# Feed-forward weights 7 and 10 in the residual rows' buffers, `wo` in four transfers: a fused attention and feed-forward block on one core

## The chip, the cores and the metric

The kernel runs on one core of a Trainium2 chip. The metric is the device time of one execution in microseconds, lower is better. The core has TensorE (PE in the profile), VectorE (DVE), ScalarE (ACT), GpSimd (POOL) and SyncE (SP), which here only issues transfers; ACT issues some transfers too. Every engine works through its own instructions in order.

## The reference

With `x` of 2048 rows by 512 columns, 32 heads of width 16, and F = 1792:

```
xn  = layernorm(x)
q, k, v = split(xn @ wqkv)                  # 512 x 1536
s   = softmax over 8 keys (rows t, t-2, ..., t-14) of q.k / 4, applied to v, then @ wo
g   = silu(relu(xn @ w1 + b1)^2 @ w2 + b2)  # w1 512 x 1792, w2 1792 x 512
out = x + s * g
```

All inputs and the output are float32; `wqkv`, `wo`, `w1` and `w2` are read from HBM once.

## The kernel before, in words

**Precision.** A matmul operand is kept as two parts, a rounded high part and the low remainder. `split` makes them: a copy on ACT (`high`) and a subtraction on the engine that is named (`low`). A product is three matmuls: high by high, high by low, low by high (`PASSES`).

**First stage (to about 136 us).** The 16 row tiles are normalised and transposed, and q, k and v are computed and stored to HBM scratch (`sq`, `sk`, `sv`). A generator, `attention`, runs the windowed attention on DVE beside everything else: eight units of 256 rows, loaded on ACT's queue (`start`, `load_u`), multiplied and reduced in pieces of about 2.3 us, and stored by SP to scratch `so` (`store`). The v tile of a unit is overwritten with the result, so ACT issues the load of the next unit's v only when that store has landed.

**Order.** Two clocks, one for PE and one for DVE, are advanced at build time by the cost of each traced instruction. `pump(margin)` traces pieces of attention until DVE's clock reaches PE's plus the margin; `defer` and `flush` put loads at a PE time. Compute instructions keep the traced order on their engine. Transfers issued through the plain `dma` on SP are not held to the traced order: a scheduler places them, each with a semaphore wait for its buffer. All transfers share eight semaphores in turn, whichever queue issues them, so a transfer also waits until the one eight before it has landed.

**Second stage (from about 136 us).** The feed-forward block runs in four chunks `c` of 512 rows. Hidden columns come in 14 blocks `f` of 128. `up(c, f)` is 12 matmuls into a PSUM tile `ph` (two buffers, `psH`), then on ACT a relu, a square rounded to `h`'s high part, and a square in full. In chunk 0 and for `f` 2 to 11, the full square goes back into `ph` and DVE makes `h`'s low part from it (`lowh`), which is what frees the `ph` buffer for `up(c, f + 2)`. `down` adds block `f - 2` into four accumulators `pb`.

**Weights.** In chunk 0 each block's weights must still be made. `load_w(f)` fetches raw `w1` and `w2` columns of block `f` into two tiles of tag `z` (four buffers, so two blocks' worth). `next_w`, called once after each `up(0, f)`, splits the next block: two copies on ACT, two subtractions on POOL; then it calls `load_w` for the block two further on, into the buffers that the subtractions free. Blocks 0 to 4 are split in the first stage, block 5 after `up(0, 2)`, block 13 after `up(0, 10)`.

**Output.** `wo` is fetched raw into two tiles `rwo` of tag `oT` (rows in an order that suits 32-column transposes) and split into `wot`. `load_o(u, force)` reads unit `u` of the attention back as `oq` in eight transfers of 64 KB. `trans_o` transposes a tile of it on DVE into PSUM, ACT copies the high part into `oT`, and `lowo` makes the low part on DVE. `out_product` is the 12 matmuls with `wot`. `gate` applies silu; `finish` multiplies and adds the residual rows `xr`, which `load_r` fetched into two buffers of tag `xr`. In chunk 0 the two `oT` tiles take the buffers of the two `rwo` tiles, and `xr` is not used before block 9.

The pool `p2`, with the tags `wot`, `oT`, `oq`, `xr` and the weight tiles of blocks 11 to 13, is opened after the pools of the first stage are closed and lies where they lay. In the profile nearly all compute instructions have line L91, the helper that records them, so tiles tell them apart; transfers have lines of their own: L404 and L405 `load_w`, L986 `wo`, L922 `load_o`, L954 `load_r`, L339 `store`, L104 the ordered queue.

Of the kernel before, what the change touches and what calls it, by code (L numbers as in the profile page):

```python
# [9 lines left out]
F32 = mybir.dt.float32  # L10
# [5 lines left out]
P = 128  # L16
S = 2048
D = 512
F = 1792
KT = D // P  # L20
NF = F // P
# [20 lines left out]
HOME = {0: 10, 1: K0, 2: T1, 3: T2, 4: T3, 5: Q0, 6: Q1, 7: K1, 8: T4, 9: V0, 10: V1}  # L42

SEVEN = range(4, 16, 2)
VSEVEN = range(6, 14, 2)

WARM = 18
# [12 lines left out]
def body(ctx: ExitStack, tc: tile.TileContext, x, wqkv, wo, w1, b1, w2, b2, out):  # L60
# [34 lines left out]
    PE, V, A, G = Ordered(nc.tensor, "PE"), Ordered(nc.vector, "V"), Ordered(nc.scalar), Ordered(nc.gpsimd)  # L95
# [4 lines left out]
    dma = nc.sync.dma_start  # L100

    def queue(out, in_):

        tc.keep_in_program_order(dma(out, in_))  # L104
# [19 lines left out]
    def piece(name):  # L124
        return keep.tile([P, 512], F32, name=name, tag="z", bufs=4)

    def high(hi, lo, src):
        A.activation(hi, src, AF.Copy)

    def low(hi, lo, src, eng):  # L130
        eng.tensor_sub(lo, src, hi.bitcast(F32))

    def split(hi, lo, src, eng):
        high(hi, lo, src)
        low(hi, lo, src, eng)
# [20 lines left out]
    def buffer(name, i):  # L156
        return wts.tile([P, 2, 2, 512], FR, name=name, tag=f"b{i}")
# [87 lines left out]
    def flush(t):  # L245
        while behind and (t is None or behind[0][0] <= t):
            behind.pop(0)[1]()
# [137 lines left out]
    def pump(margin=-SLACK):  # L385

        limit = clock["PE"] + margin
        flush(clock["PE"])
        while True:
            if coming[0] is None:  # L390
                coming[0] = next(stream, None)
            if coming[0] is None or clock["V"] + coming[0] > limit:
                break
            coming[0] = next(stream, None)
        if coming[0] is None:
            not_before(limit)
# [2 lines left out]
    w12 = {}  # L399

    def load_w(f):
        r1, r2 = (piece(f"{n}{f}") for n in ("w1r", "w2r"))
        send = queue if f < 2 else dma
        send(r1.rearrange("p (k c) -> p k c", c=P), w1[:, f * P:(f + 1) * P].rearrange("(k p) c -> p k c", p=P))  # L404
        send(r2, w2[f * P:(f + 1) * P, :])  # L405
        raws[f] = r1, r2

    def next_w():

        f = len(w12)  # L410
        if f < NF:
            w12[f] = buffer(f"w{f}", HOME[f]) if f in HOME else p2.tile([P, 2, 2, 512], FR, name=f"w{f}")
            for i, r in enumerate(raws.pop(f)):
                split(w12[f][:, 0, i], w12[f][:, 1, i], r, G)
            if f + 2 < NF:
                load_w(f + 2)


    NT = S // P
# [316 lines left out]
    for a in range(2, NT, 2):  # L736
        n, t = {2: 2, 4: 1}.get(a, 0), a + 2
        seven = t in SEVEN
        for i in (t, t + 1):
# [25 lines left out]
    for i in range(2):  # L765
        at(4, i, load_w, i)
# [28 lines left out]
    def pair_of_seven(a):  # L795

        b, last = a + 1, a + 2 == NT
        seven = a in VSEVEN
        for s in (1, 2, 0):
# [80 lines left out]
    for a in range(2, NT, 2):  # L880
        if a >= TPC:
            for t in (a, a + 1):
                queue(sx[t // TPC][:, :, t % TPC], xts[t].bitcast(F32))
        (pair_of_seven if a in SEVEN else pair)(a)
        if a == NT - 4:
# [6 lines left out]

    p2 = ctx.enter_context(tc.tile_pool(name="p2", bufs=1))
    pws, gs, pbs = {}, {}, {}

    def begin(c, j):

        pbs[c, j] = psA(f"pb{c}_{j}")
        A.activation(pbs[c, j], b2t, AF.Copy)
# [12 lines left out]
    def load_o(u, force):  # L912

        if u in oqs or (done_units[0] <= u and not force):
            return
        while done_units[0] <= u:
            flush(None)
            pump(clock["V"] - clock["PE"] + 4000)
        oqs[u] = p2.tile([P, UP // 64, 2, 2, CH], F32, name=f"oq{u}", tag="oq")
        for g in range(GR):  # L920
            src = so[g, u * UP:(u + 1) * UP, :].rearrange("(b p e) c -> p b (e c)", p=32, e=2)
            dma(oqs[u][32 * (g // 2):32 * (g // 2) + 32, :, g % 2].rearrange("p b e c -> p b (e c)"), src)  # L922
# [29 lines left out]
    def load_r(t):  # L952
        xrs[t] = p2.tile([P, D], F32, name=f"xr{t}", tag="xr", bufs=2)
        dma(xrs[t], tile_rows(x, t))  # L954
# [9 lines left out]
    wot = p2.tile([P, 2, 4, 512], FR, name="wot")  # L964
    rwo = {}

    for c in range(NCH):
        last = c == NCH - 1
        if c == 0:
            for j in range(TPC):  # L970
                begin(c, j)
        pb = [pbs[c, j] for j in range(TPC)]
        t0 = c * TPC
        room = ROOM if c else ROOM0
        for f in range(2, NF):
            up(c, f)
            if c == 0:
                next_w()
            pump()
            if c == 0 and f in (3, 6):  # L980

                i = f // 6
                rwo[i] = p2.tile([P, 2, D], F32, name=f"rwo{i}", tag="oT", bufs=2)
                for q in range(4):
                    rows = wo[q * P + 64 * i:q * P + 64 * i + 64, :].rearrange("(g p) n -> p g n", g=2)
                    dma(rwo[i][32 * q:32 * q + 32], rows)  # L986
            if c == 0:
                if 6 <= f < 10:
                    split(wot[:, 0, f - 6], wot[:, 1, f - 6], rwo[(f - 6) // 2][:, (f - 6) % 2], G)
            elif f == 2:  # L990
                finish(t0 - 4, G)
            elif f == 3:
                finish(t0 - 3, G)
                load_r(t0 - 2)
                load_r(t0 - 1)
                trans_o(t0 - 2, psT(f"pT{t0 - 2}"))
                trans_o(t0 - 1, psT(f"pT{t0 - 1}"))
            elif f == 4:
                lowo(t0 - 2)
                lowo(t0 - 1)  # L1000
            elif f == 5:
                out_product(t0 - 2, psT(f"pw{t0 - 2}"))
            elif f == 6:
                finish(t0 - 2, G)
                out_product(t0 - 1, psT(f"pw{t0 - 1}"))
            elif f == 7:
                finish(t0 - 1, G)
            if f == 2 and c:
                load_o(c * 2 - 1, True)
            elif f >= 7:  # L1010
                load_o(c * 2, f >= 9)
            if f in (9, 10) and not last:
                load_r(t0 + f - 9)
            if f == 10:
                for i in range(2):
                    trans_o(t0 + i, psT(f"pT{t0 + i}"))
            if f == 11:
                for i in range(2):
                    lowo(t0 + i)
            if f == 11 or (last and f > 11):  # L1020
                load_o(c * 2 + 1, f > 12)
            downs = [f - 2]
            if last and f == NF - 1:
                downs = []
            elif not last and f > NF - 3:
                downs = [f - 3, f - 2] if f == NF - 1 else []
            for i in downs:
                for j in range(TPC):
                    down(pb, i, j)
            pump(room)  # L1030
            lowh(f)
        out_product(t0, psT(f"pw{t0}"))
        if last:
            out_product(t0 + 1, psT(f"pw{t0 + 1}"))
        pump(room)
        if not last:
            for j in range(TPC):
                for i in range(2):
                    down(pb, NF - 2 + i, j)
                pump(room if j < 2 else -SLACK)  # L1040
                gate(c, j, pb)
                begin(c + 1, j)
            for i in range(2):
                up(c + 1, i)
                pump(ROOM)
                lowh(i)
                load_o(c * 2 + 1, False)
            out_product(t0 + 1, psT(f"pw{t0 + 1}"))
            pump(ROOM)
        else:  # L1050
            for i in range(2, TPC):
                trans_o(t0 + i, psH(f"pT{t0 + i}"))
            for i in range(2, TPC):
                lowo(t0 + i)
            xl = xTa.tile([P, TPC, 512], F32, name="xlast", tag="xT")
            dma(xl.rearrange("p (h e) n -> p h (e n)", e=2),
                x[t0 * P:(t0 + TPC) * P, :].rearrange("(h p e) n -> p h (e n)", p=P, e=2))
            for j in range(TPC):
                for f in range(NF - 3, NF):
                    down(pb, f, j)  # L1060
                gate(c, j, pb)
                if j < 2:
                    finish(t0 + j, V, xl[:, j])
            for j in range(2, TPC):
                n = D // 2 if j == TPC - 1 else D
                for i in range(0, D, n):
                    cols = slice(i, i + n)
                    out_product(t0 + j, (psT if i else psH)(f"pw{t0 + j}_{i}"), cols)
                    finish(t0 + j, V, xl[:, j], cols)
# [21 lines left out]
```

## Time and profile before

| | |
|---|---|
| Median of 3 runs | 485.32 us (484.97 to 486.93) |
| Profiled execution | 485.13 us, of which the span is 483.1 us |
| Granted TensorE clock | 1.000 |
| Busy share of the span: PE, DVE, ACT, POOL | 99%, 88%, 50%, 47% |
| Data moved | 81.47 MB, mean 169 GB/s |

The page gives the busy time of each engine, the chain of work that ended last, and groups of instructions by tile. Times in the views are microseconds from the start of the span. The profiled execution's own time is 2.0 us more than its span; the steps below are counted against the profiled execution.

### The profile page before, as it was taken

What the parts mean: (1) busy time and instruction counts of PE and PEld (TensorE: products, weight loads), DVE (VectorE), ACT (ScalarE), POOL (GpSimd) and SP (SyncE); (2) the same over time, 40 slices, a digit from 0 to 9 for tenths busy, and PEclk for the clock granted to TensorE, in tenths of its full rate; (3) what the DMA queues carried; (4) which work ended last, traced back from release to release, by engine and by line L of the source; (5) the groups of instructions that cost most, each with busy time, mean ns of one, the idle gap of its engine ahead of it and who ended that gap; (6) DMA issues with size and microseconds to landing.
All of it is one profiled execution on the core that took longest, in us unless ns stands there. A gap on an engine that the chain in (4) does not pass through costs nothing.

```text
span 483.1 us, 6128 instructions
## 1 busy us (share of the span) xinstructions
PE 477.4 (99%) x2190; PEld 396.6 (82%) x2190; DVE 423.0 (88%) x352; ACT 240.0 (50%) x441; POOL 225.3 (47%) x178
## 2 busy tenths in 40 slices
PE   8999999999999999999999999999999999999996
PEld 5888888888888888888888888888888888888885
DVE  5978999899499899999999999999999999889133
ACT  5548798856566565273513345342234543423240
POOL 1459853116986699436543322434433345253210
PEclk9999999999999999999999999999999999999999
DMA  7899999998779996571627548071707725220321
GB/s 283 243 251 258 277 243 302 263 306 269 209 198 228 255 224 151 178 166 43 170 72 185 115 164 190 26 189 43 197 16 196 224 48 145 43 86 27 87 105 71
DMA packets 71002, 81.47 MB, mean 169 GB/s; under 512 B 6204, under 2 KB 55612, under 8 KB 70972
## 3 DMA queue, kind: packets, MB, share of 16 engines
q1 hardware_dynamic: 65788, 54.87, 41.3%
q10 hardware_dynamic: 5184, 26.22, 21.8%
q8 instruction: 17, 0.28, 0.2%
q14 instruction: 13, 0.11, 0.1%
HBM read 50.60 MB, written 27.32 MB: 161 GB/s over the span
## 4 chain that ended last, share of the span: by engine, by line
PE 98%; DMA 1%; DVE 0%; POOL 0%; issue 0%; ACT 0%; POOLq 0%
PE ph L91 32%; PE pb L91 32%; PE pm L91 12%; PE pq L91 9%; PE pw L91 9%; PE pv L91 4%; DMA x<-in_A_x 1%; PE pxT L91 0%; DVE z L91 0%; DVE st L91 0%; POOL rs L91 0%; DVE xn L91 0%; ACT xT0f L91 0%; DVE mv L91 0%; DVE rs L91 0%
## 5 line engine op out<-in xcount | busy, mean ns | idle before, releaser
L91 PE MATMUL pb<-w,h 128*128 128x512 f32 x672 | 160.1, 389 | 0.0
L91 PEld LDWEIGHTS pb<-w,h 128*128 128x128 f32 x672 | 126.1, 188 | 26.2
L91 POOL TENSOR_TENSOR h<-hf,h 128x512 fp32r<-128x512 f32 x46 | 67.7, 1473 | 157.5 <-ACT hf L91 157.5
L91 PE MATMUL ph<-xU,w 128*128 128x512 f32 x504 | 120.2, 389 | 0.0
L91 ACT ACTIVATE ph<-ph,b1t 128x512 f32<-128x512 f32 x56 | 37.0, 661 | 153.9 <-PE ph L91 144.0
L91 PEld LDWEIGHTS ph<-xU,w 128*128 128x128 f32 x504 | 94.6, 188 | 19.6
L91 DVE TENSOR_TENSOR pr<-k,q 128x2048 f32<-128x2048 f32 x32 | 78.7, 2460 | 3.2 <-DMA q<-sq 2.5
L91 DVE TENSOR_TENSOR pv<-v,L 128x2048 f32<-128x2048 f32 x32 | 77.3, 2417 | 3.8 <-POOL L L91 3.1
L91 DVE TENSOR_REDUCE L<-pr 128x128 f32<-128x2048 f32 x32 | 73.0, 2281 | 0.7
L91 DVE TENSOR_REDUCE v<-pv 128x256 f32<-128x2048 f32 x32 | 72.9, 2279 | 0.7
L91 PE MATMUL pw<-wot,oT 128*128 128x512 f32 (+1 forms) x204 | 45.9, 376 | 0.0
L91 PEld LDWEIGHTS pw<-wot,oT 128*128 128x128 f32 x204 | 36.8, 188 | 7.1
L91 POOL TENSOR_TENSOR w<-w1r,w 128x512 fp32r<-128x512 f32 x14 | 31.6, 2259 | 23.4 <-ACT w L91 23.2
L91 PE MATMUL ph<-xT,w 128*128 128x512 f32 x168 | 40.0, 389 | 0.0
L91 PEld LDWEIGHTS ph<-xT,w 128*128 128x128 f32 x168 | 31.5, 188 | 6.6
L91 PE MATMUL pm<-wq,S 128*128 128x512 f32 x144 | 36.8, 392 | 0.0
L91 ACT ACTIVATE h<-ph 128x512 fp32r<-128x512 f32 x56 | 33.5, 599 | 1.8
L91 PE MATMUL pq<-wq,xT 128*128 128x512 f32 x132 | 30.9, 393 | 0.0
L91 PEld LDWEIGHTS pm<-wq,S 128*128 128x128 f32 x144 | 26.2, 188 | 5.3 <-DVE S L91 0.4
L91 PEld LDWEIGHTS pq<-wq,xT 128*128 128x128 f32 x132 | 24.5, 188 | 5.9 <-ACT xT L91 0.7
L91 ACT ACTIVATE hf<-ph 128x512 f32<-128x512 f32 x46 | 27.4, 595 | 1.9 <-POOL h L91 1.9
L91 PE MATMUL pm<-wq,xt 128*128 128x512 f32 x108 | 27.6, 392 | 0.0
(96 smaller groups left out, 531.0 us busy)
## 6 DMA issues: line engine op xcount, KB each, us to landing
k<-sk ACTq DMA_DIRECT2D x8, 960.0 KB, 7.1
v<-sv ACTq DMA_DIRECT2D x8, 960.0 KB, 7.4
sx<-xt SPq DMA_DIRECT2D x12, 512.0 KB, 5.8
xU<-sx ACTq DMA_DIRECT2D x12, 512.0 KB, 5.9
x<-in_A_x SPq DMA_DIRECT2D x16, 256.0 KB, 6.4
sk<-stg SPq DMA_DIRECT2D x8, 512.0 KB, 4.3
sq<-stg SPq DMA_DIRECT2D x8, 512.0 KB, 7.5
sv<-stg SPq DMA_DIRECT2D x8, 512.0 KB, 5.0
```

The lines of the kernel that those rows point to most:

```text
L91: return tc.keep_in_program_order(f(*a, **k))
```

## The change

Five edits, all for chunk 0 of the second stage:

- Raw weights of blocks 7 and 10 get tiles of tag `xr` in place of tag `z`. Block 7 is fetched as soon as `p2` is open, block 10 after the split of block 7.
- The order of the fetches in `next_w` follows from that: up to block 4, the split of `f` is followed by the fetch of `f + 2`; splits 5 to 9 are followed by the fetch of `f + 3` (8 to 12), split 10 by none, split 11 by block 13.
- `wo` comes in four transfers of 256 KB over 128 partitions in place of eight of 128 KB over 32 partitions. Each has a hand-written source pattern: 4 groups, 32 rows, 512 elements. The second tile is fetched at block 5 in place of 6.
- `wo` is split at blocks 9, 10 and 11 (one, one and two quarters) in place of one quarter at each of 6 to 9.
- The first `load_o` is tried from block 9 (forced from 10) in place of 7 (9); the first two `trans_o` move from block 10 to 12 and their `lowo` from 11 to 13.

```diff
+SPARE = 7, 10
...
     def load_w(f):
-        r1, r2 = (piece(f"{n}{f}") for n in ("w1r", "w2r"))
+        spare = f in SPARE
+        r1, r2 = (p2.tile([P, 512], F32, name=f"{n}{f}", tag="xr", bufs=2) if spare else piece(f"{n}{f}")
+                  for n in ("w1r", "w2r"))
...
-            if f + 2 < NF:
-                load_w(f + 2)
+            after = f + (2 if f < SPARE[0] - 2 or f > 10 else 3)
+            if after < NF and f != 10:
+                load_w(after)
...
     p2 = ctx.enter_context(tc.tile_pool(name="p2", bufs=1))
     pws, gs, pbs = {}, {}, {}
+    load_w(SPARE[0])
...
-            if c == 0 and f in (3, 6):
+            if c == 0 and f in (3, 5):
-                i = f // 6
+                i = f // 5
                 rwo[i] = p2.tile([P, 2, D], F32, name=f"rwo{i}", tag="oT", bufs=2)
-                for q in range(4):
-                    rows = wo[q * P + 64 * i:q * P + 64 * i + 64, :].rearrange("(g p) n -> p g n", g=2)
-                    dma(rwo[i][32 * q:32 * q + 32], rows)
+                for g in range(2):
+                    row = wo[64 * i + 32 * g:64 * i + 32 * g + 1, :]
+                    dma(rwo[i][:, g], bass.AP(tensor=row.tensor, offset=row.offset, ap=[[P * D, 4], [D, 32], [1, D]]))
             if c == 0:
-                if 6 <= f < 10:
-                    split(wot[:, 0, f - 6], wot[:, 1, f - 6], rwo[(f - 6) // 2][:, (f - 6) % 2], G)
+                for q in {9: (0,), 10: (1,), 11: (2, 3)}.get(f, ()):
+                    split(wot[:, 0, q], wot[:, 1, q], rwo[q // 2][:, q % 2], G)
...
-            elif f >= 7:
-                load_o(c * 2, f >= 9)
+            elif f >= (7 if c else 9):
+                load_o(c * 2, f >= (9 if c else 10))
...
-            if f == 10:
+            if f == (10 if c else 12):
                 for i in range(2):
                     trans_o(t0 + i, psT(f"pT{t0 + i}"))
-            if f == 11:
+            if f == (11 if c else 13):
                 for i in range(2):
                     lowo(t0 + i)
```

## The prediction

> **What bounds the kernel now.** I read the page first, then who PE waited for, then the chain of waits in order of time.
>
> ```profile
> PE 477.4 (99%) x2190; PEld 396.6 (82%) x2190; DVE 423.0 (88%) x352; ACT 240.0 (50%) x441; POOL 225.3 (47%) x178
> ...
> PE 98%; DMA 1%; DVE 0%; POOL 0%; issue 0%; ACT 0%; POOLq 0%
> ```
> ```profile
> PE warm L91 <- POOL mhalf L91: 1.4, 1, 1.4
> PE pxT L91 <- DVE xn L91: 0.3, 1, 0.3
> PE pq L91 <- ACT xT0f L91: 0.2, 1, 0.2
> ```
> ```profile
> 5.78 0.46 PE pxT L91 x2
> ...
> 163.59 2.72 PE ph L91 x12
> ...
> 169.03 2.72 PE ph L91 x12
> ...
> 179.91 2.72 PE ph L91 x12
> ...
> 190.79 5.44 PE ph L91 x24
> ...
> 201.67 2.72 PE pw L91 x12
> 204.39 5.44 PE pb L91 x24
> ...
> 473.67 5.60 PE pw L91 x36
> ```
>
> PE runs without a break from 5.78 us to 479.27 us (473.67 + 5.60). Its waits sum to 1.9 us, all of them in kinds of instruction that belong to the start. The change adds and removes no matmul, so it can gain nothing where it acts: the profiled execution's 485.13 us (0.2 us under the median of the runs shown, 485.32) is the floor for it. The question is only whether one of the things that are just in time for PE becomes late. Blocks of the chain that I use: `up(0, 7)` starts at 163.59, 8 at 169.03, 10 at 179.91, 12 at 190.79, 13 at 193.51, and the first output product at 201.67.
>
> What stands close to PE in this stage is read from the windows and the timelines.
>
> ```profile
> 136.00:158.00 22.00, 22.00 (x99) 18.21 (x98) 19.76 (x13) 13.86 (x26) 15.46 (x10) 1.00 0.95 231
> 158.00:180.00 22.00, 22.00 (x99) 18.22 (x98) 21.47 (x12) 13.79 (x25) 19.11 (x11) 1.00 1.01 241
> 180.00:201.00 21.00, 21.00 (x94) 17.41 (x93) 20.79 (x16) 10.49 (x19) 16.80 (x10) 1.00 0.58 152
> ```
>
> The last two columns are the share of the DMA engines and GB/s. From 136 to 180 us the 16 DMA engines have no free time (0.95, 1.01), and DVE has almost none (21.47 of 22). So a transfer that takes longer on an engine delays what is queued behind it there.
>
> **The edits with cover.** First those whose cost I put at nothing.
>
> ```profile
> 142.88 0.37 SPq L404 DMA_DIRECT2D w1r<-in_B_w  x1
> ...
> 145.68 1.41 SPq L986 DMA_DIRECT2D rwo<-in_A_wo  x3
> ...
> 150.14 4.60 SPq L986 DMA_DIRECT2D rwo<-in_A_wo  x2
> 155.12 0.57 SPq L339 DMA_DIRECT2D so<-v  x1
> 157.01 0.38 SPq L404 DMA_DIRECT2D w1r<-in_B_w  x1
> ...
> 180.38 0.33 SPq L405 DMA_DIRECT2D w2r<-in_B_w  x1
> ```
> ```profile
> SPq L986 <- DMA sq<-stg: 1.1, 1, 1.1
> ```
> ```profile
> w1r<-in_B_w SPq DMA_DIRECT2D x14, 256.0 KB, 4.3
> w2r<-in_B_w SPq DMA_DIRECT2D x14, 256.0 KB, 3.6
> ...
> rwo<-in_A_wo SPq DMA_DIRECT2D x8, 128.0 KB, 9.2
> ```
>
> Block 7's fetch. In the trace of before the first transfer into `p2` is the first `rwo`, and it waited for the store `sq<-stg` of the first stage until 145.68. Block 7's raw tiles are now the first into `p2`, so I expect them at about 145.7 and not at 142.88: later, though the edit asks for earlier. Landed after 4.3 us they are there at 150.0, after 9.2 us, as `rwo` did in the same stage, at 154.9.
>
> ```profile
> 151.73 0.62 ACT L91 ACTIVATE w<-w1r 128x512 fp32r<-128x512 f32 x1
> ...
> 161.98 0.52 ACTq L91 DMA_DIRECT2D v<-sv  x1
> 162.61 0.66 ACT L91 ACTIVATE ph<-ph,b1t 128x512 f32<-128x512 f32 x1 [2.06 <-DMA so<-v]
> ...
> 163.79 0.59 ACT L91 ACTIVATE ph<-ph 128x512 f32<-128x512 f32 x1
> ```
> ```profile
> 158.43 2.29 DVE L91 TENSOR_TENSOR pr<-k,q 128x2048 f32<-128x2048 f32 x1 [2.46 <-DMA q<-sq]
> ...
> 166.23 0.68 DVE L91 TENSOR_TENSOR h<-ph,h 128x512 fp32r<-128x512 f32 x1
> ...
> 184.28 1.30 DVE L91 STREAM_TRANSPOSE pT<-oq 128x512 f32<-128x512 f32 x2
> ...
> 188.26 1.27 DVE L91 TENSOR_TENSOR oT<-pT,oT 128x512 fp32r<-128x512 f32 x2
> ```
>
> ACT comes to block 7's split at 151.73, so it waits 0 to 3.2 us. Queued behind it on ACT are the softmax's exponential and the next relu; DVE, which waits for the exponential, sits idle 2.46 us for q until 158.43 anyway. Value taken 0; without that cover about 1 us. Blocks 8 to 12 are fetched one step of 5.44 us (169.03 to 163.59) ahead of before, which only adds slack.
>
> The `wo` splits (one copy and one subtraction each, four of them) move from blocks 6 to 9 to blocks 9 to 11.
>
> ```profile
> 186.13 1.29 POOL L91 TENSOR_TENSOR wot<-rwo,wot 128x512 fp32r<-128x512 f32 x1
> ...
> 188.43 1.30 POOL L91 TENSOR_TENSOR w<-w1r,w 128x512 fp32r<-128x512 f32 x1
> ...
> 199.97 2.83 POOL L91 TENSOR_TENSOR h<-hf,h 128x512 fp32r<-128x512 f32 x1 [1.82 <-ACT hf L91]
> ```
>
> POOL does the same four subtractions of 1.29 us, now behind block 13's weights, and has done them some 5 us after `up(0, 11)` ends at 188.07, that is by 193; they are read at 201.67. Cost 0.
>
> Transposes two blocks later. In before they ran at 184.28, 1.65 us after `up(0, 10)` ended (179.91 + 2.72 = 182.63). Behind `up(0, 12)`, which ends at 193.51, they run at about 195.2 to 196.5; `lowo` follows `up(0, 13)`, end 196.23, and is done by about 199. The product that reads it starts at 201.67, so 2.7 us are left of 13. The two `oT` copies of ACT then stand ahead of the last relu and squares of the chunk, and delay POOL's subtraction of block 13 (end 202.80) by up to 1.5 us; PE reads that at 205.5 (204.39 + five matmuls of 2.72 / 12: three of block 12 for the first accumulator, two of block 13). Cost 0; if DVE is 3 us behind, the product waits, 1 to 3 us. The eight `oq` transfers move ten us later with their readers and leave the full stage; `xr` is needed in chunk 1 only.
>
> **The edit without cover: `wo`.** No transfer of before shows how the new one runs: its source pattern starts with a dimension of 4 (the four groups of rows), where all others start with 14 or more. Bounds. From below, it runs like `w2r`, 256 KB in rows of 2 KB, 3.6 us, spread evenly, and four such are no more work than the eight of before: cost 0, and four issues less on SP (the eight took 9.2 us each to land). From above, it is spread along its outermost dimension, over four of the 16 engines. At 241 GB/s an engine moves 15.1 kB a us; 262 kB on four engines is 65.5 kB each, 4.35 us a transfer and 17.4 us for four, against 4.35 us for all eight of before. That is 13.0 us more on four engines that have nothing free.
>
> The Trainium skill, in DMA: Bandwidth & Descriptors, under "Why a DMA increments its semaphore by 16 and not by 1", says that a transfer runs on the largest number of engines up to 16 that divides the slowest dimension of both patterns, which would be 4 here. No row above can show it. The same page's Rules for kernel authors speak for the edit, one transfer over 128 partitions in place of several over a part of them; by that alone the sum would be 0.
>
> I take the upper spread, because in the code the four groups are the dimension that a split would cut first. What is late then? The store of attention unit 0 (`so<-v`, issued at 155.12) stands behind `wo` on the same queue. ACT stops at the load of the next v until that store has landed; in before this ended at 161.9 and cost ACT 2.06 us. Ahead of the store stood five of the eight `wo` transfers, 5 x 0.54 = 2.7 us of each engine; now at least the first pair, 8.7 us, so 6.0 us more, and block 9's weights, before at 157.01 and now a step earlier, 2.2 us more. The store lands at 161.9 + 8.2 = 170.1 us. From the issue of v, ACT's last square of block 6 ends 2.4 us later (163.79 + 0.59 - 161.98), and DVE's `lowh`, 0.68 us, frees `ph` at 170.2 + 3.1 = 173.3. `up(0, 8)` wants it at 169.03: PE waits 4.3 us. Without the weights' share it is 2.1 us; with the second pair ahead of the store as well, 8.7 us more, 13.0. On the other path, block 13's weights: before, their `w1` half was ready at 189.73 for 193.51, 3.8 us of slack, so 13.0 us more on four engines cost at most 9.2 there, and the wait at block 8 already covers part of it. PE's later work follows at its own pace and nothing later gives time back. Sum: 485.13 + 4.3 = 489.4 us.
>
> **The rivals.**
>
> Hidden, not slower: the `wo` transfers are spread over all engines, or over four that run faster while the other twelve rest, and the store lands before about 165.8, from where it decides (165.8 + 0.1 + 3.1 = 169.0). For it: in the next window the share is 0.58. Against: 1.01 at the store. PE stays unbroken, 485.1 us. The first half of this is also the case in which the change does what it says and relieves the queue.
>
> Late transposes: even with `wo` harmless, the oT low part comes after 201.67 because DVE runs behind the plan by more than 2.7 us; it was 1.65 behind at 184.28. PE waits 1 to 3 us at the product: 486 to 488, taken 487.6.
>
> Faster: would need a break of PE that the profiled execution does not show; 485.1 less at most 1.9 us of waits at the start, which the change doesn't touch.
>
> **How the numbers follow.** A difference of 0.5% (2.4 us) is about what a measurement of this kernel can tell from no change. Four engines and a stall, likeliest, 489.4: 0.66, of which 0.04 stays under 2.4 us. Hidden, 485.1: 0.29. Late transposes, 487.6: 0.04, three quarters of it over the bound. Faster: 0.01. So slower 0.65, within 0.5% 0.34, faster 0.01. The range must hold both main cases: it starts at 484.8, a little under the fastest run of before (484.97), and ends at 494.3, the 9.2 us of the second path; the 13.0 us of a second pair ahead of the store is left out. The likeliest case alone is 487.2 (2.1 us) to 494.3.
>
> **What would show it.** Right: `rwo` lands far later than 9.2 us; ACT waits for `so<-v` to about 170; the first break in PE is at `ph` around 169 us, released by DVE's `h`; DVE's `h<-ph,h` of block 6 is late by the same. A late block 7 shows as ACT at `w` for `w1r` around 152. Wrong: PE unbroken with ACT's wait for `so<-v` near 2 us, or the first break elsewhere, at `pw` (transposes), or at `ph` for POOL's `w` (weights).

## The result and the profile after: 497.5 us, 2.5% slower

The changed kernel takes 497.5 us (median of 6 runs, 496.15 to 500.95) against 485.43 us of before in the same series (484.97 to 486.93): a ratio of 1.0251, 95% interval 1.0215 to 1.0286. Slower, as forecast, but by 12.1 us where 4.3 were forecast, and above the range. The profiled execution took 497.22 us, its span 495.4 us, 12.3 more than before's 483.1. Transfers now have the lines L407 and L408 (`load_w`), L991 (`wo`), L340 (`store`), and the helper is L92.

The page of after: engines, DMA packets, and the chain that ended last; below it, before's DMA packets.

```profile
PE 480.3 (97%) x2190; PEld 397.5 (80%) x2190; DVE 425.7 (86%) x352; ACT 239.5 (48%) x441; POOL 232.6 (47%) x178
...
DMA packets 70890, 81.47 MB, mean 164 GB/s; under 512 B 6092, under 2 KB 55500, under 8 KB 70860
...
PE 84%; DMA 6%; DVE 4%; issue 3%; ACT 2%; SPq 0%; ACTq 0%; POOL 0%; DVEq 0%; POOLq 0%
```
```profile
DMA packets 71002, 81.47 MB, mean 169 GB/s; under 512 B 6204, under 2 KB 55612, under 8 KB 70972
```

PE's 98% of the chain has become 84%. Who PE waits for (total, times, longest), and its timeline, with the waits in brackets:

```profile
PE ph L92 <- DVE h L92: 9.1, 4, 2.8
```
```profile
159.14 3.03 PE L92 MATMUL ph<-xT,w 128*128 128x512 f32 x12 [1.04 <-DVE h L92]
...
167.51 3.01 PE L92 MATMUL ph<-xT,w 128*128 128x512 f32 x12 [2.62 <-DVE h L92]
...
175.88 4.60 PE L92 MATMUL ph<-xT,w 128*128 128x512 f32 x12 [2.64 <-DVE h L92]
...
205.15 3.06 PE L92 MATMUL ph<-xT,w 128*128 128x512 f32 x12 [2.80 <-DVE h L92]
```

Four breaks, 9.1 us, all at `ph` and all released by DVE's low part `h`: at `up(0, 6)`, 7, 8 and 13. Besides, `up(0, 8)` took 4.60 us where its neighbours show 3.0: a further 1.6 us in which PE was busy but slow. The rest of the 12.3 us is some tenths at the matmuls after the breaks. So the place that was forecast (block 8, released by `h`) is one of four. What is late ahead of them is seen on ACT, after first and then before's load of the same q:

```profile
146.76 0.62 ACT L92 ACTIVATE w<-w2r 128x512 fp32r<-128x512 f32 x1
155.90 0.52 ACTq L92 DMA_DIRECT2D q<-sq  x1
156.53 0.66 ACT L92 ACTIVATE ph<-ph,b1t 128x512 f32<-128x512 f32 x1 [9.15 <-DMA w2r<-in_B_w]
...
172.70 0.52 ACTq L92 DMA_DIRECT2D v<-sv  x1
173.32 0.66 ACT L92 ACTIVATE ph<-ph,b1t 128x512 f32<-128x512 f32 x1 [10.71 <-DMA so<-v]
```
```profile
147.77 0.52 ACTq L91 DMA_DIRECT2D q<-sq  x1
```

ACT stands twice. The second stand is the one that was forecast: v is issued only when unit 0 is stored, at 172.70 (before 161.98). The first was not: ACT's load of unit 1's q (issued at 147.77 before) waits until 155.90 for a fetch of weights, with which q shares neither a tile nor a tensor. What the two share is a semaphore (in the trace both carry the same one): the eight go round in turn over all transfers of both queues, and q's turn now comes behind block 8's `w2`. In before it came behind block 7's `w2`, which landed at 147.75, 0.02 us ahead of the issue.

SP issues the transfers; the second column is how long the issuing took:

```profile
145.96 1.98 SPq L408 DMA_DIRECT2D w2r<-in_B_w  x2
147.99 1.88 SPq L991 DMA_DIRECT2D rwo<-in_A_wo  x3
149.98 3.97 SPq L407 DMA_DIRECT2D w1r<-in_B_w  x1
154.05 3.44 SPq L408 DMA_DIRECT2D w2r<-in_B_w  x1
157.55 2.66 SPq L991 DMA_DIRECT2D rwo<-in_A_wo  x1
160.30 0.59 SPq L340 DMA_DIRECT2D so<-v  x1
```

Behind the first three `wo` transfers the next three issues (two of weights and the fourth `wo`) take 2.66 to 3.97 us each, where that of a `w1r` took 0.38 in before. The store is issued at 160.30 (before 155.12), and lands at 172.6. The windows (last columns: granted clock, share of the DMA engines, GB/s):

```profile
136.00:158.00 22.00, 22.00 (x98) 17.98 (x96) 17.96 (x10) 10.17 (x20) 12.84 (x8) 1.00 0.83 215
158.00:180.00 22.00, 15.70 (x60) 12.13 (x60) 14.51 (x10) 10.08 (x19) 12.25 (x8) 0.92 0.71 177
```

The engines together are less busy than before (0.83 and 0.71 for 0.95 and 1.01), and yet what is behind them lands later: that is what a transfer on few of them looks like. The packet counts say how few: 112 small packets (under 512 B) are gone, 6092 for 6204. A transfer that ends with one such packet on each of its engines gives just that: 8 x 16 for the old ones less 4 x 4. The times at which the trace sees the semaphores raised say the same. Each old `wo` transfer raises its semaphore in 16 steps, each new one in five: one as it is issued and four when its data land. The first three new ones land at 158.51, 163.61 and 167.08 us, 10.5 to 17.7 us after their issue (9.2 before). Of the 16 steps of block 9's `w1r`, issued at 149.98 right behind them, 12 are done by 156.83 and the last four come at 166.92 to 167.73; of unit 0's store 12 by 164.02 and the last four at 171.84 to 172.60. So a part of each transfer behind `wo`, four steps of 16, waits for `wo`, and a transfer counts as landed only with its last step.

### The profile page after: what moved, and what is told of

Its sections match the earlier page's. It is cut to its first block, busy times and chain, and to the rows that moved or that the text cites. A ratio compares the mean times of both kernels' runs of the same rounds, so it can differ in the third digit from the quotient of the medians.

```text
span 495.4 us, 6127 instructions
## 1 busy us (share of the span) xinstructions
PE 480.3 (97%) x2190; PEld 397.5 (80%) x2190; DVE 425.7 (86%) x352; ACT 239.5 (48%) x441; POOL 232.6 (47%) x178
## 2 busy tenths in 40 slices
DMA packets 70890, 81.47 MB, mean 164 GB/s; under 512 B 6092, under 2 KB 55500, under 8 KB 70860
## 4 chain that ended last, share of the span: by engine, by line
PE 84%; DMA 6%; DVE 4%; issue 3%; ACT 2%; SPq 0%; ACTq 0%; POOL 0%; DVEq 0%; POOLq 0%
PE pb L92 25%; PE ph L92 25%; PE pm L92 11%; PE pq L92 9%; PE pw L92 9%; PE pv L92 4%; DMA so<-v 2%; DMA rwo<-in_A_wo 2%; DVE L L92 1%; DVE v L92 1%; DMA sq<-stg 1%; DVE h L92 1%; DVE pv L92 1%; ACT ph L92 1%; DMA x<-in_A_x 1%
## 5 line engine op out<-in xcount | busy, mean ns | idle before, releaser
L92 PE MATMUL pb<-w,h 128*128 128x512 f32 x672 | 160.2, 389 | 0.0
L92 PEld LDWEIGHTS pb<-w,h 128*128 128x128 f32 x672 | 126.2, 188 | 26.2
L92 POOL TENSOR_TENSOR h<-hf,h 128x512 fp32r<-128x512 f32 x46 | 67.1, 1458 | 155.6 <-ACT hf L92 151.0
L92 PE MATMUL ph<-xU,w 128*128 128x512 f32 x504 | 120.3, 390 | 0.0
L92 ACT ACTIVATE ph<-ph,b1t 128x512 f32<-128x512 f32 x56 | 37.0, 661 | 170.5 <-PE ph L92 142.5
L92 PEld LDWEIGHTS ph<-xU,w 128*128 128x128 f32 x504 | 94.7, 188 | 19.6
L92 DVE TENSOR_TENSOR pv<-v,L 128x2048 f32<-128x2048 f32 x32 | 80.9, 2528 | 3.8 <-POOL L L92 3.1
L92 DVE TENSOR_TENSOR pr<-k,q 128x2048 f32<-128x2048 f32 x32 | 77.7, 2427 | 3.7 <-DMA q<-sq 3.0
L92 DVE TENSOR_REDUCE L<-pr 128x128 f32<-128x2048 f32 x32 | 73.0, 2281 | 0.7
L92 DVE TENSOR_REDUCE v<-pv 128x256 f32<-128x2048 f32 x32 | 72.9, 2278 | 0.7
L92 PE MATMUL ph<-xT,w 128*128 128x512 f32 x168 | 42.4, 405 | 9.1 <-DVE h L92 9.1
L92 PEld LDWEIGHTS ph<-xT,w 128*128 128x128 f32 x168 | 32.3, 195 | 17.8 <-DVE h L92 11.0
L92 PE MATMUL pw<-wot,oT 128*128 128x512 f32 (+1 forms) x204 | 46.0, 377 | 0.0
L92 PEld LDWEIGHTS pw<-wot,oT 128*128 128x128 f32 x204 | 36.8, 188 | 7.1
L92 POOL TENSOR_TENSOR w<-w1r,w 128x512 fp32r<-128x512 f32 x14 | 25.8, 1842 | 33.6 <-ACT w L92 33.4
L92 PE MATMUL pm<-wq,S 128*128 128x512 f32 x144 | 36.7, 392 | 0.0
L92 ACT ACTIVATE h<-ph 128x512 fp32r<-128x512 f32 x56 | 33.5, 599 | 1.7
L92 PE MATMUL pq<-wq,xT 128*128 128x512 f32 x132 | 30.9, 393 | 0.0
L92 PEld LDWEIGHTS pm<-wq,S 128*128 128x128 f32 x144 | 26.1, 189 | 5.2 <-DVE S L92 0.2
L92 PEld LDWEIGHTS pq<-wq,xT 128*128 128x128 f32 x132 | 24.5, 188 | 5.8 <-ACT xT L92 0.7
L92 ACT ACTIVATE hf<-ph 128x512 f32<-128x512 f32 x46 | 27.4, 595 | 1.5 <-POOL h L92 1.5
L92 PE MATMUL pm<-wq,xt 128*128 128x512 f32 x108 | 27.6, 392 | 0.0
```

What stands on the lines that cost most here:

```text
L92: return tc.keep_in_program_order(f(*a, **k))
```

## The experiments

Three theories came from these lines. **Turn**: ACT stands at q because the order of the transfers has shifted the turn of the semaphores. **Four engines**: `wo` on four engines holds up SP and what is behind it. **Late**: with the transposes gone from blocks 10 and 11, something else is ahead of block 11's low part on DVE. In the expectations of the first four kernels, theory Q is the turn and theory F the four engines. Each kernel was compared with before on the same chip; ratios have their 95% interval.

### Parts of the change taken out of after

**Eight transfers of `wo` again**, at blocks 3 and 5, everything else as in after.

```diff
-                for g in range(2):
-                    row = wo[64 * i + 32 * g:64 * i + 32 * g + 1, :]
-                    dma(rwo[i][:, g], bass.AP(tensor=row.tensor, offset=row.offset, ap=[[P * D, 4], [D, 32], [1, D]]))
+                for q in range(4):
+                    rows = wo[q * P + 64 * i:q * P + 64 * i + 64, :].rearrange("(g p) n -> p g n", g=2)
+                    dma(rwo[i][32 * q:32 * q + 32], rows)
```

> The changed kernel with wo in the eight transfers of before (32 partitions each), at blocks 3 and 5. Theory F: store of unit 0 on time, 485.5 to 489, the rest being what ACT still waits at the issue of q. Theory Q: block 7's fetch is still there, 493 or more.

Measured 492.06 us, 1.0130 (1.0078 to 1.0183). The breaks stay at blocks 6, 7 and 13 (1.49, 1.39 and 2.80 us), ACT stands 9.6 us at q, and only the break at block 8 is gone. With them 5.4 us of the 12.1 go; 6.7 us have other causes. The time lies between the two ranges that were expected: neither theory is enough alone.

**Four flat transfers**: four of 256 KB again, each from 128 consecutive rows (other rows than the output needs).

```diff
-                    row = wo[64 * i + 32 * g:64 * i + 32 * g + 1, :]
-                    dma(rwo[i][:, g], bass.AP(tensor=row.tensor, offset=row.offset, ap=[[P * D, 4], [D, 32], [1, D]]))
+                    dma(rwo[i][:, g], wo[(2 * i + g) * P:(2 * i + g + 1) * P, :])
```

> The changed kernel with one thing different: each of the four wo transfers reads 128 consecutive rows (outermost dimension 128, wrong rows for the product), so number, size, order and semaphores of the transfers stay. Theory F (four engines: a source pattern whose outermost dimension is 4 is moved by four of the 16 DMA engines, and the attention store and the semaphores behind it wait): the store of unit 0 lands by about 165 instead of 172.7, the wait of up(0,8) is gone; what ACT waits for at the issue of q (9.15 us, for the block 8 w2 fetch) stays, and with it about 4 us at up(0,6) and up(0,7): 489, between 486 and 490. Theory Q (turn of the semaphores: block 7's fetch makes ACT's issue of q wait for a fetch that lands late; the wo pattern is harmless): 496 or more.

Measured 493.4 us, 1.0143 (1.0091 to 1.0195), with breaks at the same three places and ACT standing 8.7 us at q. The store landed at 164.26, not 172.6. The time again lies between the two expected ranges. What this kernel keeps of the loss has nothing to do with four engines, and part of it is block 13's break (2.80 us), which neither theory has.

**No spare tiles**: after with the weights fetched as in before.

```diff
-        spare = f in SPARE
+        spare = False
...
-            after = f + (2 if f < SPARE[0] - 2 or f > 10 else 3)
-            if after < NF and f != 10:
-                load_w(after)
+            if f + 2 < NF:
+                load_w(f + 2)
...
-    load_w(SPARE[0])
```

> The changed kernel with raw weights 7 and 10 back in the z buffers and the fetch order of before; wo in four transfers, late splits and late transposes stay. Theory F: the store still lands late (168 to 173), 490 to 496. Theory Q: ACT issues q without a long wait, 485 to 488.

Measured 496.84 us, 1.0226 (1.0189 to 1.0264): nearly all of the loss is left, a little above F's range and far above Q's. Q waits here too, 12.28 us, for a transfer of `wo`:

```profile
159.45 0.66 ACT L92 ACTIVATE ph<-ph,b1t 128x512 f32<-128x512 f32 x1 [12.28 <-DMA rwo<-in_A_wo]
```

The turn can be lost in more than one way, and by either edit.

**The four transfers alone** in before.

```diff
-                for q in range(4):
-                    rows = wo[q * P + 64 * i:q * P + 64 * i + 64, :].rearrange("(g p) n -> p g n", g=2)
-                    dma(rwo[i][32 * q:32 * q + 32], rows)
+                for g in range(2):
+                    row = wo[64 * i + 32 * g:64 * i + 32 * g + 1, :]
+                    dma(rwo[i][:, g], bass.AP(tensor=row.tensor, offset=row.offset, ap=[[P * D, 4], [D, 32], [1, D]]))
```

> The kernel before with nothing but the four wo transfers (fetched at blocks 3 and 6, split at 6 to 9 as before). Theory F: slower, 489 to 496, the first break of PE at ph around block 7 or 8. Theory Q: 485 to 486, as before.

Measured 494.43 us, 1.0175 (1.0142 to 1.0207): +9.0 us. Its timelines of PE and ACT, and a window:

```profile
162.04 5.49 PE L91 MATMUL ph<-xT,w 128*128 128x512 f32 x12 [4.10 <-DVE h L91]
```
```profile
158.80 0.52 ACTq L91 DMA_DIRECT2D q<-sq  x1
159.43 0.66 ACT L91 ACTIVATE ph<-ph,b1t 128x512 f32<-128x512 f32 x1 [12.21 <-DMA rwo<-in_A_wo]
```
```profile
162.00:168.00 6.00, 5.96 (x14) 4.71 (x15) 1.34 (x3) 2.42 (x5) 2.34 (x2) 0.50 0.73 189
```

ACT stands 12.21 us at q, PE breaks 4.10 us, and then runs at a granted clock of 0.50: 14 matmuls in 6 us (0.43 us each) where 28 are usual. With the slow matmuls behind it PE ends up 7.2 us later, not 4.1. The time is inside F's range, but the first break comes through q, at block 6: the pattern and the turn act together here. No break is at block 13, and the transposes are at block 10 here: the late theory's first sign.

### One part alone

**The spare tiles and the order of the fetches alone**: `wo` as in before, splits at 6 to 9, transposes at 10 (the first two of the five edits of the change).

> The kernel before with the spare weight buffers and the new order of the weight fetches only; wo in its eight transfers at blocks 3 and 6, splits and transposes where they were. Theory of the semaphore's turn: the extra fetch of block 7 moves ACT's load of unit 1's q onto the semaphore that the fetch of block 8's w2 raised, ACT stands some 9 us before that load (w2r<-in_B_w as the releaser), PE breaks 1 to 3 us at ph around 160 and 167, none at 200; 488.5 to 490 us. Theory of wo on four engines alone: wo is as before, so 485.5 us and no break. Theory of the late transposes alone: they are where they were, 485.5 us.

Measured 487.82 us (487.19 to 490.18), 1.0052 (1.0032 to 1.0072): +2.4 us. ACT and PE:

```profile
156.81 0.52 ACTq L92 DMA_DIRECT2D q<-sq  x1
157.44 0.66 ACT L92 ACTIVATE ph<-ph,b1t 128x512 f32<-128x512 f32 x1 [7.29 <-DVE v L92]
```
```profile
167.26 3.04 PE L92 MATMUL ph<-xT,w 128*128 128x512 f32 x12 [0.96 <-DVE h L92]
```

ACT again stands before q, 7.29 us. (The row names DVE's `v`, but q was issued 0.02 us after block 7's `w2`, whose turn it follows here, had landed at 156.79; a releaser is inferred, and this one had long been done.) PE breaks by 0.96 us and then loses some three tenths at each of three later blocks. The profiled execution took 490.18 us, the longest of its ten: PE was 2.7 us behind before's already by 68 us, ahead of anything that was changed, and the times in these rows stand that much later. Behind that, PE loses 2.5 us, which fits the median's 2.4. The turn is right in mechanism, with a smaller price than expected.

**The late part alone**: splits at 9 to 11, `load_o` from 9, transposes at 12, low parts at 13.

> The kernel before with the late part only: wo splits at blocks 9 to 11, load_o from block 9, the first transposes at 12 and their low parts at 13; weights and the fetch of wo as before. Theory of the late transposes: with the transposes gone from blocks 10 and 11, one more piece of attention is traced ahead of block 11's low part on DVE, ph comes free late and PE breaks 2 to 3 us at ph around 200 us; 487.5 to 488.5 us, and nothing breaks before. Rival, that the break at 200 to 205 in the other runs was only what the earlier breaks left behind: PE unbroken, 485.4 us.

Measured 489.77 us, 1.0084 (1.0052 to 1.0116): +4.3 us, above the expected range, which had the break but not the slow matmuls. One break, and slow matmuls behind it; on DVE, first before, then this kernel:

```profile
195.83 4.60 PE L91 MATMUL ph<-xT,w 128*128 128x512 f32 x12 [1.88 <-DVE h L91]
```
```profile
191.80 0.68 DVE L91 TENSOR_TENSOR h<-ph,h 128x512 fp32r<-128x512 f32 x1
```
```profile
186.57 2.78 DVE L91 TENSOR_TENSOR pv<-v,L 128x2048 f32<-128x2048 f32 x1
...
189.88 2.27 DVE L91 TENSOR_REDUCE v<-pv 128x256 f32<-128x2048 f32 x1
192.18 2.99 DVE L91 TENSOR_TENSOR pv<-v,L 128x2048 f32<-128x2048 f32 x1
195.09 0.68 DVE L91 TENSOR_TENSOR h<-ph,h 128x512 fp32r<-128x512 f32 x1
```

Block 11's low part is at 195.09, not 191.80. Ahead of it stand two attention pieces more, 2.27 and 2.99 us, less the 2.6 us of transposes and low parts that left; the other pieces run some tenths longer (2.78 us for a `pv` that took 2.42). `pump` saw DVE's planned clock free up and put whole pieces there. `up(0, 13)`, due at 193.5, waits.

**One more transfer**: before with a 2 KB fetch behind the first of `wo`.

```diff
                     dma(rwo[i][32 * q:32 * q + 32], rows)
+                    if i == 0 and q == 0:
+                        pad = p2.tile([16, 32], F32, name="pad")
+                        dma(pad, wo[:16, :32])
```

> The kernel before with one more transfer, 2 KB (16 rows of 32 columns of wo, read by nobody), right behind the first transfer of wo. Theory of the semaphore's turn: one transfer more shifts the turn by one, so that ACT's load of unit 1's q follows the first transfer of wo, landed about 154.4, and not block 7's w2, landed 147.75: ACT stands about 7 us at that load, PE breaks at ph around 158 to 167; 486.5 to 489 us. Rival, that what counts is the load on the DMA engines: 2 KB are nothing, 485.4 us and no wait of ACT.

Measured 488.0 us (487.08 to 490.6), 1.0052 (1.0033 to 1.0072). This run did not test what it was made for: the scheduler moved a later `wo` transfer back by one, q kept its place in the turn and was issued at 147.96. PE had no break in this stage.

```profile
PE 479.7 (99%) x2190; PEld 396.9 (82%) x2190; DVE 425.2 (88%) x352; ACT 240.0 (49%) x441; POOL 228.4 (47%) x178
```

The same 2190 matmuls were busy 479.7 us instead of 477.4: in four stretches of some 25 us they ran 2% to 3% slower. Neither theory gives this. Set beside before's matmul by matmul, the slow ones are those of `up` and `down` for blocks 11, 12 and 13 and a few next to them, the same in all four chunks, 2.2 us together; all others of this stage keep their pace. In the code these are the blocks whose weight tiles are taken from `p2` after `pad`, which is 128 bytes wide. That points at where these tiles lie as the reason; no run moves them alone, so it is not shown, and why a matmul should mind stays open.

### Causes taken away

**`wo` held back** in after, to blocks 6 and 7, by a write on POOL that the transfers must wait for.

```diff
-            if c == 0 and f in (3, 5):
+            if c == 0 and f in (6, 7):
-                i = f // 5
+                i = f // 7
...
+                G.memset(rwo[i][:, :, :1], 0.0)
```

> The changed kernel with the two wo tiles fetched at blocks 6 and 7, and held there by a write of one column on POOL just before the fetch (the column is then overwritten by the fetch). Theory of the semaphore's turn: the load of unit 1's q then follows a transfer that landed by 146, so ACT's wait of 9 us at q goes, and with it the PE breaks around 159 and 167; the store of unit 0 no longer stands behind wo, so the break around 176 goes too; left is the break of 2 to 3 us at 200 to 205 from the late transposes: 487 to 489 us, more by 1 to 3 if wo on four engines now holds something later. Rival, that spare weights or four engines cost by themselves whatever the order of the transfers: 492 us or more.

Measured 490.54 us, 1.0094 (1.0066 to 1.0121), above the 487 to 489 that were expected and below the rival's 492. ACT's loads and PE:

```profile
145.78 1.15 ACTq L92 DMA_DIRECT2D q<-sq  x1
160.38 0.52 ACTq L92 DMA_DIRECT2D v<-sv  x1
```
```profile
186.09 3.06 PE L92 MATMUL ph<-xT,w 128*128 128x512 f32 x12 [0.85 <-DVE h L92]
...
197.03 4.60 PE L92 MATMUL ph<-xT,w 128*128 128x512 f32 x12 [2.44 <-DVE h L92]
```

Q goes at 145.78 and v at 160.38, earlier than before's. The breaks at 6, 7 and 8 are gone with both stands of ACT; what is left is 0.85 us at block 11, whose cause was not followed, and the late part's break with its slow matmuls. Spare tiles and a four-engine `wo` cost next to nothing where nothing is due behind them.

**The late part with less room for the planner**: as in the kernel with the late part alone, and

```diff
-            pump()
+            pump(-SLACK - (2500 if c == 0 and f in (10, 11) else 0))
...
-            pump(room)
+            pump(room - 2500 if c == 0 and f in (10, 11) else room)
             lowh(f)
```

> The late part alone, as before, but the planner's margin is 2.5 us less at blocks 10 and 11 of chunk 0, which is what the two transposes and two low parts took there: DVE then makes blocks 10's and 11's low parts two pieces of attention earlier. Theory that the planner filled the free place with attention and so made block 11's low part late: the PE break of 1.9 us at 195.8 and the slow matmuls behind it go, 485.4 to 486.5 us. Rival, that the late wo splits and transposes take the time themselves (POOL, ACT's copies, or DVE slowed beside POOL): a break stays at 193 to 205, 488 us or more.

Measured 485.63 us, 1.0000 (0.9975 to 1.0025): all 4.3 us are gone, with splits, transposes and low parts as late as in after. Block 11's low part is now at 190.06, where DVE waits for ACT, and PE runs through:

```profile
185.23 2.28 DVE L91 TENSOR_TENSOR pv<-v,L 128x2048 f32<-128x2048 f32 x1
190.06 0.69 DVE L91 TENSOR_TENSOR h<-ph,h 128x512 fp32r<-128x512 f32 x1 [2.55 <-ACT ph L91]
```
```profile
190.76 5.60 PE L91 MATMUL ph<-xT,w 128*128 128x512 f32 x24
```

**Four engines without the lost turn**: before with the four transfers, and the residual rows' fetches, which the scheduler had put between them, held back on POOL.

```diff
         xrs[t] = p2.tile([P, D], F32, name=f"xr{t}", tag="xr", bufs=2)
+        if t < 2:
+            G.memset(xrs[t][:, :1], 0.0)
         dma(xrs[t], tile_rows(x, t))
```

> The kernel before with wo in the four transfers on four engines, and the residual rows' fetches held back until blocks 9 and 10 by a write of one column on POOL, so that two transfers fewer stand ahead in the turn and the load of unit 1's q follows block 7's w2 (landed about 147) and not a transfer of wo. Theory of the turn: ACT's wait of 12.2 us at q goes, q is issued by 148 to 149, and the break of 4.1 us at 162 goes; 486 to 491 us, what is left being a late store of unit 0 behind SP's slow issues. Theory of four engines alone (what is queued behind wo is late, whatever the turn): q's data are then late in the queue, the break at 162 stays, 493 to 495 us.

Measured 492.29 us, 1.0132 (1.0091 to 1.0173): 2.1 us less than the four transfers alone (494.43, of the other series), and above the range of the turn's expectation, below that of the four engines alone. ACT and PE:

```profile
147.60 0.52 ACTq L91 DMA_DIRECT2D q<-sq  x1
...
168.21 0.63 ACT L91 ACTIVATE w<-w1r 128x512 fp32r<-128x512 f32 x1 [11.03 <-DMA w1r<-in_B_w]
...
170.22 0.52 ACTq L91 DMA_DIRECT2D v<-sv  x1
```
```profile
173.40 5.48 PE L91 MATMUL ph<-xT,w 128*128 128x512 f32 x12 [4.45 <-DVE h L91]
```

The turn's half is confirmed: q goes at 147.60 and the break at 162 is gone. But four engines break PE by themselves, once, at block 8: 4.45 us and 2.6 us of slow matmuls.

**The four flat transfers alone** in before: the order and the turn of the four alone, on 16 engines (the edit is that of the flat transfers above).

> The kernel before with wo in four transfers of 128 consecutive rows each (other rows than the output needs), on 16 engines, and nothing else. The order of the transfers and the turn are those of the four on four engines alone (494.4 us). Theory of the turn alone: ACT waits for a transfer of wo before q again, landed about 153 to 154 now, some 6 to 7 us, and PE breaks 0 to 2 us: 486 to 490 us. Theory of four engines: SP's issues take 0.4 us each again and not 3.3, nothing is late: 485.4 us. Rival, that four large transfers ahead of the rest cost as much on any engines: 493 us or more.

Measured 489.46 us (488.23 to 490.72), 1.0070 (1.0049 to 1.0091): +3.8 us, inside the turn's range. ACT stands 9.15 us at q for a transfer of `wo`, and PE breaks at blocks 6 and 7 by 1.04 and 1.34 us. So the turn costs this with 16 engines too. SP's issues of the four, first of the kernel with the residual rows held (four engines), then of this one:

```profile
145.52 7.99 SPq L988 DMA_DIRECT2D rwo<-in_A_wo  x4
153.55 3.45 SPq L404 DMA_DIRECT2D w1r<-in_B_w  x1
157.13 3.01 SPq L405 DMA_DIRECT2D w2r<-in_B_w  x1
160.23 0.60 SPq L339 DMA_DIRECT2D so<-v  x1
```
```profile
146.08 2.69 SPq L985 DMA_DIRECT2D rwo<-in_A_wo  x4
...
149.34 0.70 SPq L404 DMA_DIRECT2D w1r<-in_B_w  x1
```
```profile
DMA packets 70938, 81.47 MB, mean 167 GB/s; under 512 B 6140, under 2 KB 55548, under 8 KB 70908
```

The same bytes in as many transfers, and 2.69 us of issues instead of 7.99. Here 64 small packets are gone against before, 4 x 16: four transfers less on 16 engines each. That closes the count of four.

**After with both cures**: `wo` held back, and less room at blocks 10 and 11 (the two diffs above together).

> The changed kernel with wo held back to blocks 6 and 7 and the planner's margin 2.5 us less at blocks 10 and 11. If the turn with the four engines, and the attention piece ahead of block 11's low part, are all that the change costs, the breaks at 159 to 176 and at 197 are gone, and the 0.85 us at 186 is left: 485.5 to 487 us. If something else of the change costs (the later wo, the spare tiles by themselves): 489 us or more.

Measured 486.32 us (485.15 to 488.05), 0.9998 (0.9976 to 1.0020), inside the expected range; the interval leaves room for about 1 us either way.

```profile
PE ph L92 <- DVE h L92: 0.9, 1, 0.9
```

Spare tiles, four transfers, late splits and late transposes are all still there, only `wo` is fetched later and the planner has less room at two blocks, and the loss is gone but for the 0.85 us at block 11. So the causes of the 12.1 us are found; and no version is faster than before, since PE has nothing to win there.

## Why the prediction was right or wrong

**The floor: right.** No kernel with any part of the change was measurably faster than before, and the two that cured a cause came back to 1.0000 and 0.9998 of it.

**Four engines: right, and by the count.** The Trainium skill's rule (DMA: Bandwidth & Descriptors, "Why a DMA increments its semaphore by 16 and not by 1") gave four engines for this source pattern; the packets that went missing, 112 and 64, and the four late steps of each semaphore agree with four. The sentence that the sum would be 0 by that page's rules for authors went too far: the Trainium skill (DMA: Bandwidth & Descriptors, "Rules for kernel authors") does advise one transfer over 128 partitions, but another row of the same table says that an outermost dimension under 16 confines a transfer to at most that many engines, which is this case. Where nothing else is in the way, the predicted chain came out almost to the tenth: in the kernel with the residual rows held, v is issued at 170.22 (forecast: the store lands at 170.1), `up(0, 8)` starts at 173.40 (173.3), and PE breaks by 4.45 us (4.3). Part of that is luck, for the way there differs. The prediction went by bytes queued on four full engines, and counted SP only in its lower bound, as four issues fewer. It put the first pair of `wo` ahead of the store at 4.35 us each; all four were ahead, but they landed at 157.90, 161.07, 164.04 and 167.36, about 3.2 us apart. And the runs show SP itself held, 7.99 us for four issues. ACT waits 11.03 us for block 8's weights, issued at 153.55 (148.49 before) and there but for their last four steps by 159.88; those come by 168.18, behind `wo`. The store adds 1.35 us behind that.

**Block 7's fetch: right in itself, wrong in what it moved.** It was forecast for 145.7 and for landing between 150.0 and 154.9; `w1r` went at 145.54 and landed at 149.99, `w2r` at 154.65, and the split, which ACT reached at 158.23 only, waited for nothing. The step that failed is "Value taken 0; without that cover about 1 us", with "Blocks 8 to 12 are fetched ... ahead of before, which only adds slack": ACT's loads stand in the same turn of eight as SP's fetches, a rule that the document had told in its description of the order, and the added fetch put q behind another one. Alone that cost 2.4 us. The four transfers do the same to q in another way, 12.21 us of ACT's time. That is why the parts do not add up: 2.4, 4.3 and 9.0 us make 15.7, and the whole is 12.1.

**Transposes two blocks later: wrong at the step "Cost 0", and the rival looked at the wrong place.** The product at 201.67, which it priced at 1 to 3 us with a chance of 0.04, never waited. What came late is `up(0, 13)`, 4.3 us by itself, since leaving DVE's place empty made the planner put attention pieces there. The `wo` splits cost nothing, as forecast: they are as late in the kernel with less room, at 1.0000.

**Not in the sum at all: the clock.** A break of PE was priced at its length. Behind 2.64 us in after, `up(0, 8)` took 1.6 us more than its neighbours; behind 4.10 and 4.45 us elsewhere 2.6 more.

**The total.** 4.3 us was right for the mechanism that it named, taken alone and without the clock. The other two mechanisms and the clock make the rest: in after PE is 4.2 us behind before's with block 7 (q's load), 8.7 with block 8 (the store, and the slow matmuls) and 12.0 with block 13 (the late part). By the prediction's own signs its path was there (`wo` landing late, ACT at `so<-v`, the break at block 8), but the first break, which it put around 169 us, came at 159.14, at block 6. The range ended at 494.3 on the two paths that were priced; it had no room for ACT's other load.

## What to carry to other kernels

Where transfers share semaphores in turn, adding, merging or dropping a transfer is an edit to every later load on every queue: list what each later transfer will follow, above all loads that a compute engine issues, since that engine then stands. Where a planner fills the time that a moved step leaves, price what it puts there, a whole piece at a time, and not only the step that moved. And look at the slowest dimension of a transfer's source pattern: of two transfers of the same bytes here, the one with 4 ran on four engines and the one with 128 on sixteen, and only the first held the queue.

## What was not expected of the hardware

- An issue on SP is not always cheap. With three or four 256 KB transfers outstanding that run on four engines, the single issues behind them, of weights and of a `wo`, took 2.66 to 3.97 us in after (0.38 for a `w1r` in before); behind four of the same size on 16 engines 0.70. In that time the DMA engines as a whole were half idle; first the kernel with the residual rows held, then before:

```profile
156.00:162.00 6.00, 6.00 (x29) 4.95 (x28) 4.45 (x3) 1.15 (x3) 0.00 (x0) 1.00 0.48 156
```
```profile
156.00:162.00 6.00, 6.00 (x28) 4.99 (x27) 3.57 (x3) 2.48 (x5) 2.01 (x2) 1.00 1.09 300
```

The share is 0.48, where before had 1.09 in the same six us. Why an issue waits then, no run shows.

- PE at half clock after a break of about 2 us. In the kernel with the late part alone, eight matmuls behind a break of 1.88 us started 0.427 us apart instead of 0.227 (granted clock 0.53 from 197.0 to 200.5 us), and then the clock came back. Breaks of 2.80 us, in after and in after with eight transfers, were followed by none. The Trainium skill (TensorE: Matmul & The Clock Gate, "Why this matters for your kernels") warns of idle gaps over about 3 us, and says under "What's actually happening" that the window runs freely. The half rate and a penalty that comes and goes agree with that; the length does not, 1.88 us was enough here, and the measurement decides.
